# Block-causal attention and a gated MLP on one core: the order of every engine's steps is played out in the source

## The chip, the cores and the metric

The kernel runs on one core of a Trainium2 chip. The metric is the device time of one execution in microseconds (us); the comparison is with the kernel before the change. The core has five engines that run side by side, each through its own list of instructions, strictly in the order in which the program lists them: PE (TensorE, matrix products), DVE (VectorE), ACT (ScalarE), POOL (GpSimd), and SP (SyncE), which here does nothing but start DMA transfers. An instruction that needs another engine's result waits at the head of its engine's list, and all that stands behind it waits too.

## What is computed

First an attention over 8 batches, 8 heads, 576 positions and a head size of 64, where a position sees its own block of 64 positions and all blocks before it:

```
scores = (q @ k^T) / 8 ; masked where block(key) > block(query)
p = exp(scores - rowmax) / (rowsum + 1e-9)
x = p @ v                      # heads side by side: (8, 576, 512)
```

Then a gated MLP, one batch after the other:

```
h = relu(x @ w_in)             # 512 -> 1024; u = first half, v = second half
vn = (v - mean(v)) / sqrt(var(v) + 1e-6)
vs = w_spatial @ vn + b        # 576 x 576, mixes positions
out = (u * vs) @ w_out         # 512 -> 512
```

All inputs and outputs are fp32 (the two weight matrices of the MLP come as 64-bit floats and are converted on the chip). To be exact enough on a one-pass matmul format, most operands are split into a high and a low part, and a product is three matmuls: high by high, high by low, low by high. The attention scores of batch 0 alone are taken straight in fp32.

## The kernel before, in words

**Units of work.** Heads go in pairs, so the attention is 32 pairs (8 batches by 4), numbered 0 to 31. For one pair the kernel: loads the queries and keys (`load_pair`, one buffer `raw`) and the values (`load_v`); for batches 1 to 7 splits them into `hi` and `lo` (`prep_pair`, lines 242 and 245); makes scores on PE in seven slots of query tiles (`scores` L292 and `scores_last` L306); masks each score row, takes the row's extreme and moves it from PSUM to SBUF on DVE (`rows`, L337 and L355); takes exponentials on ACT with row sums (`exps`, L367); adds 1e-9 and takes the reciprocal on DVE (`norm`, L375 and L378) and scales the rows on POOL (L380). The probabilities must then be transposed. In batch 0 PE does it (`transposes`, L402, copied by ACT in L405); later DVE transposes 32 by 32 blocks (`blocks`, L415, four calls for a pair) and 16 DMAs put the blocks in place (`regroup`, L422). The product with the values follows on PE (`av`, L459, a low and a high part), its result is split by ACT and DVE (L439, L440), and POOL copies a tail of 64 positions (L480).

**The MLP.** `moe(b)` is a list of groups of matmuls, each group ending in one PSUM bank: 5 `v_group`s (L542, L555), 8 `u_group`s (L635, relu on ACT in L642), 8 `sp_group`s (L664 to L671, multiplied into u by DVE in L673, split by ACT in L674 and POOL or DVE in L677) and 8 output groups, made two at a time (`out_groups`, L697, copied out by ACT in L705 and stored by a DMA of SP's queue in L706). Behind each v group stands a chain that normalises its rows: relu on ACT (L549), statistics on DVE (L570, L571), logarithm and exponential on ACT (L574, L575), four small steps on DVE (`refine`, L578 to L590), the scaling (L596), the high part (L610) and the low part (L620) on DVE. The spatial product needs all five chains.

**What sets the order.** Batch 0's attention is a hand-written loop over steps of slots, with the conversions of the weights strewn in between (`spread`, `step_background`). From pair 4 on, the order comes from a small clock: every matmul of the MLP advances it by 133 or 230 ns (`M_NS`, `V_NS`, `tick`), and at fixed offsets from the start of a pair (the constants `ROWS_AT` to `V_AT`) events fire that list a step on DVE, ACT, POOL or SP. The scores stand at the start of a pair's period, the last scores at 4000 ns, the value product of the pair before at 13000 ns. The offsets are the same for all pairs and do not know how long any engine other than PE is busy. This order is fixed for PE, DVE, ACT and POOL (`tc.manual_schedule`, L849).

**Buffers.** Scores have six one-bank PSUM buffers and the MLP two. There is one buffer each for raw, hi and lo, one for the transposed probabilities, two for the untransposed ones, six for x.

## Time and profile before

| what | us |
|---|---|
| median of 3 runs | 769.93 (766.99 to 770.73) |
| the profiled execution | 768.27 |
| its span, from the first to the last instruction | 766.5 |
| PE busy in the span | 689.4 (90%) |
| DVE busy | 531.2 (69%) |
| ACT busy | 377.5 (49%) |
| POOL busy | 315.3 (41%) |

The span is what the engines' records cover; 1.8 us of the profiled execution lie outside it. Matmuls are pipelined: the record of one lasts about 0.3 us while the next starts 0.13 us after it, so PE counts as busy for a while after its last matmul has started, and PE busy at 90% does not mean that 90% of the matmuls that could have been done were done. The rows of the profile name a line of the kernel, an engine, the tile written and the tiles read; "<-" ahead of a name of an engine and a line means that this ended the wait.

### The profile page before, as it was taken

How to read it: one execution, taken by the hardware profiler on the slowest of the kernel's cores; microseconds unless marked ns; L12 is line 12 of the kernel's file. 1: busy time of each engine (PE TensorE's matmuls, PEld its weight loads, DVE VectorE, ACT ScalarE, POOL GpSimd, SP SyncE). 2: the span in 40 equal slices, each digit the busy share in tenths (PEclk: the TensorE clock that was granted, in tenths of full speed). 3: DMA queues.
4: the chain of work that ended last, by engine and by line, in shares of the span. 5: the costliest groups of instructions: out<-in, count | busy, mean ns of one | idle time of the engine just before them, and what ended most of it. 6: DMA issues, size and time to landing. Idle time of an engine off the chain costs nothing.

```text
span 766.5 us, 15461 instructions
## 1 busy us (share of the span) xinstructions
PE 689.4 (90%) x5320; PEld 596.0 (78%) x5320; DVE 531.2 (69%) x1609; ACT 377.5 (49%) x1068; POOL 315.3 (41%) x481
## 2 busy tenths in 40 slices
PE   8988678699999998989988999999988998987998
PEld 5656567688788886878878887888877887976897
DVE  7966979556975689657985679757985679741641
ACT  6774455444455545535555554444555454531322
POOL 5862476433354432544444532454444423530011
PEclk9989789989999999999999999999999999999999
DMA  6531454636446554456455544456446463334001
GB/s 220 179 130 34 118 174 125 167 103 172 108 118 165 153 137 105 115 152 160 108 133 152 144 131 127 119 144 169 110 122 166 113 160 95 93 86 117 1 16 47
DMA packets 42914, 95.56 MB, mean 125 GB/s; under 512 B 9554, under 2 KB 18258, under 8 KB 42836
## 3 DMA queue, kind: packets, MB, share of 16 engines
q1 hardware_dynamic: 42836, 94.58, 45.5%
q8 instruction: 42, 0.69, 0.4%
q14 instruction: 36, 0.29, 0.1%
HBM read 39.23 MB, written 9.44 MB: 63 GB/s over the span
## 4 chain that ended last, share of the span: by engine, by line
PE 42%; DVE 26%; SPq 10%; ACT 9%; DMA 7%; issue 4%; POOL 2%; DVEq 0%; ACTq 0%; POOLq 0%
PE ms L664 10%; SPq L422 9%; PE s_avh L459 7%; PE mv L542 6%; PE mu L635 6%; DVE p L415 5%; PE s L292 4%; PE mo L697 4%; ACT p L367 3%; DVE p L337 3%; PE s_avl L459 3%; DMA outT<-o 3%; ACT hi L242 2%; DVE vl L620 2%; DVE st L570 2%
## 5 line engine op out<-in xcount | busy, mean ns | idle before, releaser
L380 POOL TENSOR_SCALAR p<-p,ssum 128x128 f32<-128x128 f32 (+5 forms) x288 | 178.9, 635 | 252.5 <-DVE ssum L378 117.0
L367 ACT ACTIVATE p<-p,nmax 128x128 f32<-128x128 f32 (+5 forms) x288 | 169.1, 588 | 83.4 <-DVE nmax L337 53.2
L635 PE MATMUL mu<-x,wi_hi 128*128 128x288 f32 x512 | 119.8, 314 | 10.5 <-ACT u L642 9.4
L415 DVE STREAM_TRANSPOSE p<-p 128x768 f32<-128x768 f32 (+1 forms) x112 | 109.7, 992 | 1.2 <-POOL p L380 1.1
L635 PEld LDWEIGHTS mu<-x,wi_hi 128*128 128x128 f32 x512 | 91.9, 203 | 16.0 <-ACT u L642 11.3
L664 PE MATMUL ms<-ws_hi,vh 128*128 128x288 f32 x256 | 80.7, 315 | 21.2 <-ACT o L705 13.9
L542 PE MATMUL mv<-wi_hi,x 128*128 128x512 f32 x256 | 88.2, 404 | 4.2 <-ACT vr L549 4.2
L697 PE MATMUL mo<-gh,wo_hi 128*128 128x288 f32 x256 | 77.0, 301 | 5.4 <-ACT o L705 4.6
L664 PE MATMUL ms<-ws_lo,vh 128*128 128x288 f32 x256 | 78.0, 305 | 0.0
L664 PE MATMUL ms<-ws_hi,vl 128*128 128x288 f32 x256 | 77.7, 304 | 0.0
L337 DVE CUSTOM_DVE_ANT_1 p<-s,mask 128x128 f32<-128x128 f32 (+1 forms) x168 | 64.1, 413 | 17.1 <-PE s L292 14.3
L697 PE MATMUL mo<-gh,wo_lo 128*128 128x288 f32 x256 | 75.6, 295 | 0.0
L697 PE MATMUL mo<-gl,wo_hi 128*128 128x288 f32 x256 | 75.5, 295 | 0.0
L459 PE MATMUL s_avh<-pt,v 128*64 128x64 f32 (+2 forms) x1152 | 75.5, 285 | 0.0
L635 PE MATMUL mu<-x,wi_lo 128*128 128x288 f32 x256 | 75.0, 312 | 0.0
L674 ACT CAST gh<-u 128x288 fp32r<-128x288 f32 x64 | 27.1, 432 | 93.7 <-DVE u L673 85.6
L677 POOL TENSOR_TENSOR gl<-u,gh 128x288 fp32r<-128x288 f32 x48 | 38.2, 803 | 81.0 <-ACT gh L674 75.4
L664 PEld LDWEIGHTS ms<-ws_hi,vh 128*128 128x128 f32 x256 | 49.8, 195 | 27.6 <-ACT o L705 16.1
L673 DVE TENSOR_TENSOR u<-ms,u 128x288 f32<-128x288 f32 x64 | 27.8, 443 | 62.3 <-PE ms L671 62.1
L459 PEld LDWEIGHTS s_avh<-pt,v 128*64 128x64 f32 x1152 | 59.7, 140 | 14.2 <-issue 1.4
L245 POOL TENSOR_TENSOR lo<-raw,hi 128x320 fp32r<-128x320 f32 (+1 forms) x84 | 63.4, 779 | 2.7 <-ACT hi L242 2.6
L542 PEld LDWEIGHTS mv<-wi_hi,x 128*128 128x128 f32 x256 | 48.5, 190 | 16.8 <-ACT vr L549 5.4
(112 smaller groups left out, 1534.4 us busy)
## 6 DMA issues: line engine op xcount, KB each, us to landing
pt<-p SPq DMA_DIRECT2D x448, 100.0 KB, 2.2
raw<-qk SPq DMA_DIRECT2D x31, 640.0 KB, 4.4
v<-v SPq DMA_DIRECT2D x32, 320.0 KB, 3.0
outT<-o SPq DMA_DIRECT2D x64, 144.0 KB, 3.0
rwi<-w_in SPq DMA_DIRECT2D x8, 512.0 KB, 3.5
rwo<-w_out SPq DMA_DIRECT2D x4, 512.0 KB, 4.1
rws<-w_spT SPq DMA_DIRECT2D x4, 288.0 KB, 2.8
raw<-qk SPq DMA_DIRECT2D x2, 192.0 KB, 3.1
```

Source lines behind the costliest of these rows:

```text
L245: (nc.vector if n == 0 else nc.gpsimd).tensor_tensor(out=lo[:, cs], in0=raw[:, cs], in1=hi[:, cs].bitcast(F32), op=ALU.subtract)
L337: nc.vector.tensor_tensor_reduce(out=out, in0=by_block(b, bk[:, o:o + n]), in1=mask0[:, 512 - n:] if b == 0 else tiles(mask, 3 - t, t + 1) ...
L367: nc.scalar.activation(out, out, AF.Exp, bias=mx, scale=-1.0, accum_out=ssum[:, r:r + 1])
L380: nc.gpsimd.tensor_scalar(out=out, in0=out, scalar1=ssum[:, 4 + r:5 + r], scalar2=1.0, op0=ALU.mult, op1=ALU.mult,)
L415: nc.vector.transpose(pp, pp)
L422: nc.sync.dma_start(dst[32 * j:32 * j + 32, i], pp[32 * i:32 * i + 32, j])
L459: nc.tensor.matmul(bank[js, q0:q1], vt[:, c, js], move(j), start=(n == 0), stop=(n == len(todo) - 1), skip_group_check=True,)
L542: nc.tensor.matmul(ps, xs[k][:, j, cs], w[:, k, DH:], start=(n == 0), stop=(n == 3 * NC - 1),)
L635: nc.tensor.matmul(ps[:, :HT], w[:, k, ds], xs[k][:, j, zs], start=(n == 0), stop=(n == 3 * NC - 1),)
L664: nc.tensor.matmul(ps[:, :HT], a[:, ds], w[:, k, zs], start=(n == 0), stop=False)
L677: ).tensor_tensor(
L697: nc.tensor.matmul(ps[ec][:, :HT], w[:, k, es], a[:, k, :], start=(k == 0 and n == 0), stop=(last and n == 2),)
```

## The change

Every step of all engines, from the first load to the last store, is first put into one list (`Line.add`) with its engine, its length in ns, the steps that must be done before it (`after`; `behind` orders without a need for the result), the buffers that it takes and those that it gives back (`Ring`, `Hold`) and a rank. Then `Line.play` walks through time: at each turn every engine names the step that it could start earliest (`pick`; among those that could start at once, the lowest rank, then the oldest), the engine with the earliest start lists its step, its length is added to the engine's clock, and the steps that needed it are told when it ends. The order in which the steps come up is the order of the program on all five engines, SP among them.

PE has four lanes, each in fixed order (`pick_pe`): A the value products, T the transposes, S the scores, M the MLP. If several can start, A goes before T, T before S, S before M; `SLACK` counts an A as startable only 3000 ns after its data are there and an S 800 ns after (both 100 ns in batch 0), an M 100 ns after. `TURN` is a price in ns for going from one kind of work on PE to another. The scores of a pair from batch 1 on are held back until the MLP has gone far enough (`gate`, `LEAD` 5 pairs ahead).

Some steps are changed beside their order:
- 1e-9 is added to the row sums by POOL (`guard`) and no more by DVE; the reciprocal stays on DVE.
- `refine`, four small steps on DVE, becomes three on POOL.
- The high part of the normalised v is copied by ACT, no more by DVE.
- Relu of u, the copies of the output and batch 0's copies of transposed blocks go to ACT or DVE, whichever comes free first in the play.
- The score slots of both heads share one PSUM tile of two banks (three such tiles for six single ones). The order of the keys is moved by one tile so that the last slot's mask and extreme are one step on DVE instead of two, and the block transposes on DVE are seven calls for a pair instead of four.
- The output groups come one at a time; between the last spatial group of a half and its output groups stands a group that needs neither, and the last four output groups of a batch come after the first v group of the next.

The diff, cut to its core:

```diff
-RUN2, LAST = 2, 5
-
-
-ROWS_AT = [1000, 2600, 4200, 5600, 7000, 8600, 11000]
-EXP_LAG = 700
-NORM_AT = [5500, 8000, 11500, 13500]
-BLOCKS_AT = [9000, 12000, 15000, 16500]
-REGROUP_AT = 17500
-SPLIT_AT = 6000, 12000
-LAST_AT, OUT_AT = 4000, 13000
-STEP = 2860
-V_AT = [700, 1900, 2900, 3700, 4500, 5300]
-EARLY = OUT_AT - 3000
-V_NS, M_NS = 230, 133
-MOE_NS = 56 * V_NS + 304 * M_NS
+LEAD = 5.0
+
+TURN = {
+    ("M", "S"): 91, ("S", "M"): 384, ("S", "T"): 260, ("T", "S"): 200, ("S", "A"): 219,
+    ("A", "S"): 200, ("A", "M"): 250, ("A", "T"): 203, ("M", "A"): 96, ("T", "A"): 96,
+}
+REACH = {"PE": 170, "DVE": 125, "ACT": 145, "POOL": 70}
+SLACK = {"A": 3000, "S": 800, "T": 0, "M": 100}
...
+    def free_at(self, ahead=0):
+        k = len(self.given) + ahead - self.bufs
+        if k < 0:
+            return 0.0
+        if k >= len(self.given) or self.given[k].users:
+            return None
+        return self.given[k].freed
...
+    def start_of(self, op):
+        if op.left:
+            return None
+        at = op.ready
+        ahead = {}
+        for h in op.takes:
+            f = h.ring.free_at(ahead.get(id(h.ring), 0))
+            if f is None:
+                return None
+            ahead[id(h.ring)] = ahead.get(id(h.ring), 0) + 1
+            at = max(at, f)
+        return at
...
+    def pick_pe(self):
+        now = self.free["PE"]
+        heads = {k: q[0] for k, q in self.lanes.items() if q}
+        at = {k: self.start_of(op) for k, op in heads.items()}
+        if self.run and at.get(self.run) is not None:
+            return max(now, at[self.run]), heads[self.run]
+        at = {k: max(now, t + (SLACK[k] if heads[k].slack is None else heads[k].slack)) for k, t in at.items() if t is not None}
+        soon = [k for k in ("A", "T", "S", "M") if k in at and at[k] <= now + 1]
+        for k in soon:
+            op = heads[k]
+            if k == "S" and op.gate is not None and self.spent < op.gate and "M" in heads:
+                continue
+            return at[k], op
+        late = [k for k in at if not (k == "S" and heads[k].gate is not None and self.spent < heads[k].gate and "M" in at)]
+        if not late:
+            return None
+        k = min(late, key=lambda k: at[k])
+        return at[k], heads[k]
...
+    def pick(self, eng):
+        if eng == "PE":
+            return self.pick_pe()
+        now, best = self.free[eng], None
+        found = []
+        for op in self.open[eng]:
+            t = self.start_of(op)
+            if t is not None:
+                found.append((max(t, now), op))
+        if not found:
+            return None
+        first = min(t for t, _ in found)
+        return min(((t, op) for t, op in found if t <= first + 1), key=lambda x: (x[1].rank, x[1].turn))
...
+    def settle(self, op, at):
+        op.done = at
+        for h in op.drops:
+            h.users -= 1
+            h.freed = max(h.freed, at)
+        for heir in op.heirs + op.trail:
+            heir.left -= 1
+            if heir in op.heirs:
+                heir.ready = max(heir.ready, at)
+            if not heir.left and not heir.lane:
+                self.offer(heir)
...
+    def play(self):
+        while True:
+            picks = [(p[0], e, p[1]) for e in self.ENGINES for p in [self.pick(e)] if p]
+            if not picks:
+                break
+            start, eng, op = min(picks, key=lambda x: (x[0], self.ENGINES.index(x[1])))
+            for h in op.takes:
+                h.ring.given.append(h)
+            if len(op.eng) > 1:
+                op.fn(eng)
+            else:
+                op.fn()
+            ns = op.ns[op.eng.index(eng)]
+            if eng == "PE":
+                self.lanes[op.lane].pop(0)
+                kind = "M" if op.lane == "S" and op.waive else op.lane
+                end = start + TURN.get((self.kind, kind), 0) + ns
+                self.kind, self.run = kind, op.first and op.lane
+                if kind == "M" and op.lane == "M":
+                    self.spent += ns
+                done = end + REACH[eng]
+            else:
+                for e in op.eng:
+                    self.open[e].remove(op)
+            if eng == "SP":
+                end = start + ns
+                self.bus = max(self.bus, start + 300) + op.size / 240
+                done = self.bus + 1300
+            elif eng != "PE":
+                end = start + ns
+                done = end + REACH[eng]
+            self.free[eng] = end
+            self.last = eng, ns
+            self.settle(op, done)
...
-    ps_s = ctx.enter_context(tc.tile_pool(name="ps_s", bufs=6, space=PSUM))
+    ps_s = ctx.enter_context(tc.tile_pool(name="ps_s", bufs=3, space=PSUM))
     ps_m = ctx.enter_context(tc.tile_pool(name="ps_m", bufs=2, space=PSUM))
...
+        s_ops = []
+        pp_hold = Hold(r_pp, 7 if first else 16)
+        pt_hold = Hold(r_pt, 1)
+        s_hold = [Hold(r_s, n) for n in (4, 2, 2, 1)]
+        ns = (640, 640, 853, 960) if first else (670, 510, 690, 885)
+        for k in range(4):
+            op = add("PE", ns[k], (lambda k=k: scores(k)) if k < 3 else scores_last, after=need[k],
+                     takes=[s_hold[k]] + ([pp_hold] if k == 0 else []), lane="S",
+                     drops=([raw_hold] if first else [hl_hold] if k == 3 else []))
+            op.first = k < 2
+            op.waive = k == 3
+            op.slack = 100 if first else None
+            if k == 0 and not first:
+                op.gate = (g - LEAD) * MOE_NS / NPAIR
+            s_ops.append(op)
+
+        runs_of = [[] for _ in range(4)]
...
+            def guard(k=k, n=n):
+                s = box["sum", k]
+                nc.gpsimd.tensor_scalar(
+                    out=s[:, 0:n], in0=s[:, 0:n], scalar1=EPS_SM, scalar2=None, op0=ALU.add
                 )
...
+            def turn(k=k, n=n):
+                s = box["sum", k]
+                nc.vector.reciprocal(s[:, 4:4 + n], s[:, 0:n])
+
+            a = add("POOL", 200, guard, after=[e for *_, e in runs_of[k]], rank=2)
+            a = add("DVE", 165, turn, after=[a], rank=1.5)
...
+                cols = (P * ((t0, t1)[r] + 1)) if hd < 2 else S if first else Q0
+                muls[i].append(add("POOL", 240 + 0.825 * cols, scale, after=[a], rank=3))
...
-    def norm(b, pr, k):
-        ssum, runs = sums.pop((b, pr, k))
-        n = len(runs)
-        nc.vector.tensor_scalar(
-            out=ssum[:, 0:n], in0=ssum[:, 0:n], scalar1=EPS_SM, scalar2=None, op0=ALU.add
-        )
-        nc.vector.reciprocal(ssum[:, 4:4 + n], ssum[:, 0:n])
-        for r, out in enumerate(runs):
-            nc.gpsimd.tensor_scalar(
-                out=out, in0=out, scalar1=ssum[:, 4 + r:5 + r],
-                scalar2=1.0, op0=ALU.mult, op1=ALU.mult,
-            )
...
+                def blocks(t0=t0, t1=t1):
+                    x = box["pp"][:, :, t0:t1, :]
+                    nc.vector.transpose(x, x)
+
+                done.append(add("DVE", 70 + 1.05 * P * (t1 - t0), blocks, after=muls[i], rank=3))
...
+                    moved.append(add("SP", 635, regroup, after=done, drops=[pp_hold], rank=2, size=102400,
+                                     behind=moved[:1],
+                                     takes=[pt_hold] if not moved else []))
...
+        al = add("PE", 646, low_product, after=[*moved, got_v], takes=[a_hold], lane="A")
+        al.first = True
+        al.slack = 100 if first else None
+        ah = add("PE", 2082, high_product, behind=[al], lane="A", drops=[pt_hold, v_hold])
...
+            def refine(n):
+                st = box["st"]
+                if n == 0:
+                    nc.gpsimd.tensor_scalar(
+                        out=st[:m, 2:3], in0=st[:m, 7:8], scalar1=EPS_LN, scalar2=st[:m, 1:2],
+                        op0=ALU.add, op1=ALU.mult,
+                    )
+                elif n == 1:
+                    nc.gpsimd.tensor_scalar(
+                        out=st[:m, 3:4], in0=st[:m, 2:3], scalar1=st[:m, 1:2], scalar2=-0.5,
+                        op0=ALU.mult, op1=ALU.mult,
+                    )
+                else:
+                    nc.gpsimd.tensor_scalar(
+                        out=st[:m, 4:5], in0=st[:m, 3:4], scalar1=1.5, scalar2=st[:m, 1:2],
+                        op0=ALU.add, op1=ALU.mult,
+                    )
...
+            a = add("DVE", 800, stats, after=[a], rank=1.2)
+            a = add("ACT", 417, root, after=[a], rank=1)
+            for n in range(3):
+                a = add("POOL", 245, lambda n=n: refine(n), after=[a], rank=1)
+            a = add("DVE", 460, scale, after=[a], rank=1.2)
...
+            h = add("ACT", 520, high, after=[a], behind=vn_done[:1], takes=takes, rank=1.4)
+            l = add("DVE", 600, rest, after=[h], drops=[vr_hold], rank=1.4)
...
+                a = add(("ACT", "DVE"), (292, 360), copy, after=[ends[ec]], takes=[o_hold], drops=[holds[ec]], rank=0)
+                add("SP", 420, store, after=[a], drops=[o_hold], rank=0, size=P * HT * 4)
...
-            after(t + ROWS_AT[i], lambda i=i: do_rows(i))
-            after(t + ROWS_AT[i] + EXP_LAG, lambda i=i: exps(b, pr, i, kept[i]))
-        for k in range(4):
-            after(t + NORM_AT[k], lambda k=k: norm(b, pr, k))
-            after(t + BLOCKS_AT[k], lambda k=k: blocks(b, pr, k))
-        after(t + REGROUP_AT, lambda: regroup(b, pr))
...
+        sp = [lambda z=z, d=d: sp_group(z, d) for z in range(2) for d in range(ND)]
+        out = [lambda z=z, e=e: out_groups(z, (e,)) for z in range(2) for e in range(NO)]
+        front = [(vs if w == "v" else us).pop(0) for w in order]
+        return front[:1], front[1:] + sp[:ND + 1] + out[:NO] + sp[ND + 1:], out[NO:]
...
+    for b in range(B):
+        for pr in range(NPAIR):
+            attention(b, pr)
+    close = []
+    for b in range(B):
+        start, middle, end = moe(b, ready)
+        for group in start + close + middle:
+            group()
+        close = end
+    for group in close:
+        group()
 
...
+        line.play()
```

1207 lines of the change are left out of this document (597 added, 610 removed).

## The prediction

> **What bounds the kernel now.** I read the busy shares first, then the busy time by stage, then the distance between matmuls, and only then who waits for whom. The profiled execution took 768.27 us, 766.5 of them in the span; the median of the three runs is 769.93, so it is an ordinary execution, and the sum below is made against 768.27. About 0.5% either way is what a measurement of this kernel can tell from no change.
>
> ```profile
> span 766.5 us, 15461 instructions
> ...
> PE 689.4 (90%) x5320; PEld 596.0 (78%) x5320; DVE 531.2 (69%) x1609; ACT 377.5 (49%) x1068; POOL 315.3 (41%) x481
> ```
>
> PE leads, with DVE next. By stages (first column the stretch, then its length and the busy time of each engine, the granted clock of PE behind them): batch 0's attention, the start of the MLP beside batch 1's attention, the even middle, and the last batch's MLP alone.
>
> ```profile
> 0.00:61.00 61.00, 53.28 (x371) 34.74 (x371) 43.77 (x153) 43.28 (x121) 39.02 (x60) 0.94 0.49 166
> 61.00:180.00 119.00, 93.61 (x679) 82.63 (x677) 89.35 (x246) 58.44 (x160) 59.95 (x80) 0.89 0.48 129
> 180.00:705.00 525.00, 484.76 (x3882) 425.25 (x3880) 375.60 (x1151) 259.72 (x745) 211.23 (x334) 0.99 0.50 131
> 705.00:766.50 61.50, 57.72 (x400) 53.42 (x396) 22.52 (x59) 16.09 (x42) 5.11 (x7) 0.99 0.07 25
> ```
>
> A busy PE is not one at its peak, so I price its work by undisturbed runs of matmuls. The first four rows are from the chain of waits, the others from the timeline.
>
> ```profile
> 491.70 2.11 PE s L292 x24
> ...
> 711.12 1.58 PE mu L635 x12
> 712.70 2.77 PE mv L542 x12
> ...
> 759.77 3.07 PE mo L697 x21
> ```
>
> ```profile
> 484.41 0.87 PE L459 MATMUL s_avl<-pt,v 128*64 128x256 f32 x8
> ...
> 487.31 0.40 PE L664 MATMUL ms<-ws_hi,vl 128*128 128x288 f32 x1
> ```
>
> ```profile
> 495.96 0.31 PE L306 MATMUL s<-hi 128*128 128x320 f32 x1
> ...
> 496.70 0.31 PE L306 MATMUL s<-hi,lo 128*128 128x320 f32 x1
> ```
>
> A v matmul costs 2.77 / 12 = 0.231 us, every other one of the MLP 1.58 / 12 = 0.132. A batch has 4 x 12 + 8 = 56 of the first and 64 groups' worth, 304, of the second: 12.9 + 40.0 = 53.0 us. A pair's attention is 2.11 for scores, six last scores at (496.70 - 495.96) / 5 = 0.148, so 0.89, and 487.31 - 484.41 = 2.90 for the value product: 5.9. Going to other work and back costs by the change's own table 91 + 384 + 96 + 250 ns; less the 0.1 already inside 2.90 I take 0.7. That makes 6.6 us a pair and 53.0 + 4 x 6.6 = 79.4 a batch.
>
> PE's floor with the first 61 us as they are: 61 + 8 x 53.0 + 28 x 6.6 + 3.7 (from the last matmul, 759.77 + 3.07, to the end) = 673.5. So 93 us of the span are PE waiting, restarting or running at a lower clock behind its first 61 us. Where they lie:
>
> ```profile
> 526.49:614.32 87.83, 80.66 (x659) 70.62 (x656) 63.64 (x197) 44.79 (x129) 36.47 (x58) 1.00 0.51 134
> ...
> sum 526.95, PE 486.71 PEld 426.97 DVE 376.02 ACT 260.40 POOL 211.23; mean PE 81.12 PEld 71.16 DVE 62.67 ACT 43.40 POOL 35.20
> ```
>
> These are stretches of four pairs, from value product to value product, and the sum of all six from 178.35 to 705.30. One takes 87.8 where 79.4 are needed; all six lose 526.95 - 6 x 79.4 = 50.6. The stretch after 705.3 loses 61.2 - (2.2 of a value product + 53.0 + 3.7) = 2.3. What is left, 93 - 50.6 - 2.3 = 40, lies in the 117 us from 61 to 178, a third of that stage. The waits of PE, for 180 to 700 and then for 62 to 180:
>
> ```profile
> PE s L306 <- DVE nmax L337: 8.9, 8, 1.8
> PE ms L664 <- ACT o L705: 8.2, 5, 3.5
> PE ms L664 <- DVE u L673: 6.6, 8, 1.1
> PE mu L635 <- ACT u L642: 4.6, 6, 1.5
> PE mo L697 <- ACT o L705: 3.9, 8, 0.7
> ```
>
> ```profile
> PE ms L664 <- ACT o L705: 5.8, 1, 5.8
> PE s L306 <- DVE nmax L337: 5.5, 3, 2.2
> PE mu L635 <- ACT u L642: 4.9, 1, 4.9
> PE s L306 <- DVE st L578: 3.9, 1, 3.9
> PE mv L542 <- ACT vr L549: 3.0, 1, 3.0
> ```
>
> None of them is a lack of an engine's time over the span: in each case PE's list asks for something that ACT or DVE has further back in its own. They add to 32.2 and 23.1 us.
>
> **The change part by part.** *The middle.* Each wait has a place in the new order. The output copies are late because their store is:
>
> ```profile
> ACT o L705 <- DMA outT<-o: 30.9, 10, 7.1
> ...
> SPq L706 <- ACT o L705: 68.9, 21, 39.6
> ```
>
> ```profile
> 490.53 10.06 SPq L422 DMA_DIRECT2D pt<-p  x16
> 500.69 1.01 SPq L706 DMA_DIRECT2D outT<-o  x2
> ```
>
> Sixteen regroup issues occupy SP for 10 us and two stores go out right behind them. In the play a store has rank 0 and regroup rank 2, 635 ns an issue, so a store passes between two of them: of 8.2 + 3.9 I take 11 back. The last scores stand at a fixed 4000 ns; the play lists them 0.8 us after their bank is read: 8 of 8.9 back. The gating product and the relu get rank 0, the second may go to DVE: 4 of 6.6 and 3 of 4.6. The 18.4 that no row names are restarts and gaps of tenths; denser lists remove few: 4. Sum 30 of 50.6. Bounds: nothing, and all 50.6. I take the inner value because the lists are fixed and every length that is off comes back as a short wait.
>
> *The first MLP.* The same causes give 15 of 23.1 back. DVE is the engine that is short here (89.35 of 119 us, with PE waiting on it while it works through weights, v chains and transposes in the written order), and the play sends weights early and takes steps off it. Needed PE work is 117 - 40 = 77 us, and at 0.89 of the clock it lasts 77 / 0.89 - 77 = 9.5 longer; with fewer long gaps I take 5 back, and 4 of the rest: 24 of 40. Bounds 0 and 40. The Trainium skill (TensorE: Matmul & The Clock Gate, Part 1) says that the clock halves after an idle window of about 3.4 us and returns after a busy one of the same length. The waits of 5.8, 4.9 and 3.9 us beside 0.89 agree; by that rule all 9.5 would return as soon as no gap reaches that length, and the sum would be 4.5 us lower.
>
> *Batch 0.* ACT, DVE and POOL are busy 43, 44 and 39 of the 61 us, so none is full, and each pair's chain runs through all of them. The copies of transposed blocks may now go to DVE, but conversions of weights move in. Bounds: nothing, and 13 (the busiest engine's 44 plus 4 until the first data); I take 5. *The end* has one output group at a time with less to wait for: 1.
>
> *Steps taken off DVE.* The rows (busy us, mean ns) of the guard, the high part and two of the four steps of `refine`, and two POOL rows, the row scalings and the nearest to a small step:
>
> ```profile
> L375 DVE TENSOR_SCALAR ssum<-ssum 128x2 f32<-128x2 f32 (+2 forms) x128 | 22.6, 176 | 10.5 <-ACT p L367 10.2
> ...
> L610 DVE CAST vh<-vr 128x512 fp32r<-128x512 f32 x32 | 15.8, 493 | 0.4
> ...
> L582 DVE TENSOR_SCALAR st<-st 128x1 f32<-128x1 f32 (+1 forms) x40 | 10.9, 271 | 9.9 <-ACT st L575 6.7 <-DVE st L578 0.5
> L586 DVE TENSOR_SCALAR st<-st 128x1 f32<-128x1 f32 (+1 forms) x40 | 8.5, 213 | 1.4
> ```
>
> ```profile
> L380 POOL TENSOR_SCALAR p<-p,ssum 128x128 f32<-128x128 f32 (+5 forms) x288 | 178.9, 635 | 252.5 <-DVE ssum L378 117.0 <-DMA pt<-p 79.8 <-ACT p L367 33.5
> ...
> L480 POOL TENSOR_SCALAR xs<-x 128x128 fp32r<-128x128 f32 x32 | 10.0, 312 | 92.5 <-DVE ssum L375 68.0 <-DVE x L440 24.3
> ```
>
> These four alone free 58 us of DVE, so it is no bound. POOL gets 128 + 120 small steps. No row shows one; the nearest, 128 columns wide, takes 0.312, and nothing is the lower bound. At 0.312 they add 77 us to 315 (51% of the span), at 0.25, which I take for a step of 1 to 4 columns, 62. This is hidden by POOL's idle 60% in the middle. What isn't free is latency: each step stands behind POOL's row scalings in its list (635 ns), three times in a v chain. In batches 1 to 7 four u groups, 4 x 1.58 = 6.3 us, cover the last chain. Bounds per batch: 0 and 3 x 0.6 = 1.8; I take 0.3, so 2 us over the program. ACT gets the 32 casts, 16 us on 49%: nothing, under PE's work; without that cover half a us for each. The last slot's single reduction and three more transposes a pair cancel on DVE.
>
> Sum: -30 - 24 - 5 - 1 + 2 = -58. The span becomes 708.5, the execution 710.
>
> **The rivals.** *Everything waits in its place.* With 45 of 50.6, 34 of 40, 8 in batch 0 and 1 at the end it is 768 - 88 = 680. For it: no engine but PE is over 70% busy. Against it: the play knows nothing of an engine's disturbances.
>
> *The shared path of DVE and POOL.* The same DVE step at two times, and what POOL did at the second:
>
> ```profile
> 73.97 0.69 DVE L620 TENSOR_TENSOR vl<-vr,vh 128x512 fp32r<-128x512 f32 x1
> ...
> 87.89 1.77 DVE L620 TENSOR_TENSOR vl<-vr,vh 128x512 fp32r<-128x512 f32 x1
> ```
>
> ```profile
> 87.71 1.41 POOL L138 TENSOR_TENSOR ws_lo<-rws,ws_hi 128x576 fp32r<-128x576 f32 x1 [2.15 <-ACT ws_hi L136]
> ```
>
> It is held until POOL's subtraction is over: 1.08 us that no length in the change contains. A batch has some 13 such steps on DVE (5 scalings, 4 low parts of v, 4 of keys) and 18 subtractions on POOL. If half are held for a us and half of that reaches PE, it is 3.3 us a batch, 26 in all: 768 - 58 + 26 = 736. Against it: most steps of the profile show no such length. The Trainium skill (GPSIMD Engine Reference, 1. Specifications) says that GpSimd shares its SBUF interfaces with VectorE and collides with instructions of two SBUF inputs or in a two-port mode; the pair of rows agrees for the first kind, and by that rule a tighter packing brings more such meetings.
>
> *SP's list becomes the bound.* SP's order was not in the old fixed lists and is in the new. A store that waits for its ACT copy between regroup issues holds the rest, and PE's value product, fixed in its list, holds the MLP behind it. The play keeps 3.0 us of slack, so lateness beyond 3.0 us costs its excess 28 times; the gain is used up at 3.0 + 62 / 28 = 5.2 us for every pair, and at 6.0 the time is 768 - 58 + 28 x 3.0 = 794. For it: stores have waited up to 39.6 us at SP's head. Against it: then the copies were late themselves.
>
> *The lengths are wrong enough* that the new order waits as often as the old: 768.
>
> **How the numbers follow.** Forecast 710: 0.49, with its own range 696 to 724 (half the 30 and 24 lost or won in part). Everything in place, 680: 0.14. Shared path, 736: 0.24. No change: 0.04. SP, 794: 0.09. Faster by over 0.5% are the first three, 0.87; same 0.04; slower 0.09. The range from 684 to 748 leaves out about half of the second case, the two on the other side and the worst of the shared path.
>
> **What would show it.** Right: a stretch of four pairs falls from 87 to about 82 us; the waits for the output copy and for the last scores' bank go; stores stand between regroup issues; the clock from 61 to 180 is above 0.93; POOL's small steps take 0.2 to 0.3 us and DVE's busy time is below 480. Wrong: waits of PE for pt (then SP), DVE steps of over 1 us in numbers (shared path), or spatial products waiting for vl or st (the chain over POOL).

## The result and the profile after

The changed kernel takes 727.02 us (median of four runs, 725.46 to 730.96) against 770.33 (766.99 to 774.55) for the kernel before in the same comparison: a ratio of 0.9443, 95% interval 0.9383 to 0.9503. It is faster by 43 us where 58 to 60 were forecast. The time lies in the range given (684 to 748), but outside the 696 to 724 that the forecast of 710 had for itself, and nearer to the rival's 736. The profiled execution took 726.69 us, 724.9 of them in the span.

The span and the busy time of each engine, from the page of the profile after:

```profile
span 724.9 us, 15406 instructions
...
PE 668.6 (92%) x5320; PEld 585.1 (81%) x5320; DVE 501.3 (69%) x1397; ACT 361.7 (50%) x1013; POOL 384.0 (53%) x727
```

DVE lost 30 us of work and POOL gained 69, but the share of DVE did not fall, since the span became shorter. By stage (length, busy time and count of PE, its weight loads, DVE, ACT and POOL, then the granted clock and the share and GB/s of DMA), first before with the stages cut where the value product of batch 0, the start of batch 1's MLP and the start of the last MLP lie, then after:

```profile
61.00:180.40 119.40, 94.01 (x688) 82.96 (x684) 89.35 (x246) 58.44 (x160) 59.95 (x80) 0.89 0.48 130
180.40:708.20 527.80, 487.56 (x3909) 427.39 (x3907) 376.02 (x1152) 260.10 (x746) 211.23 (x334) 0.98 0.50 130
708.20:766.50 58.30, 54.52 (x361) 50.95 (x360) 22.09 (x58) 15.72 (x41) 5.11 (x7) 1.00 0.06 21
```

```profile
0.00:74.75 74.75, 56.29 (x399) 39.69 (x399) 54.90 (x171) 46.44 (x131) 55.44 (x89) 0.84 0.46 148
74.75:169.40 94.65, 82.50 (x648) 72.88 (x648) 73.77 (x192) 50.57 (x138) 63.76 (x105) 0.95 0.56 152
169.40:667.80 498.40, 475.95 (x3907) 421.07 (x3907) 351.46 (x992) 251.67 (x715) 256.77 (x515) 1.00 0.53 137
667.80:724.90 57.10, 53.90 (x371) 51.45 (x369) 21.12 (x44) 13.00 (x31) 8.00 (x18) 1.00 0.09 30
```

After the change the last four output groups of a batch (4 x 12 x 0.132 = 6.4 us) stand behind the next batch's first v group, so the cuts of the second table stand 6.4 us behind those v groups: the same work lies between the cuts of both. The middle went from 527.8 to 498.4, which is 88.0 to 83.1 us a batch and a gain of 29.4. The last MLP gained 1.2, the first 119.4 - 94.65 = 24.7. Batch 0's attention takes 74.75 where it took 61: a loss of 13.7. Together 41.6, all of the span's difference.

Who PE waits for in the middle (170 to 662 us; total, times, longest):

```profile
PE mu L919 <- ACT u L932: 7.3, 4, 2.2
PE mo L1008 <- DVE u L970: 5.8, 5, 2.0
PE s L532 <- DVE nmax L574: 3.8, 5, 1.2
PE av L714 <- DMA pt<-p: 1.2, 1, 1.2
```

The wait of the spatial product for the output copy, 8.2 us before, is gone, and that for the last scores' bank fell from 8.9 to 3.8. The wait for relu rose from 4.6 to 7.3, and gating's stayed at 6.6 in all (5.8 of it now ahead of the output product, 0.9 ahead of the spatial one). SP's list shows the stores between the regroup issues (start, duration, count):

```profile
146.40 1.16 SPq L696 DMA_DIRECT2D pt<-p  x2
147.63 0.55 SPq L1026 DMA_DIRECT2D outT<-o  x1
148.23 1.14 SPq L696 DMA_DIRECT2D pt<-p  x2
```

The small steps on POOL, the guard and the three of `refine`, have these durations (busy us, mean ns, idle before them):

```profile
L623 POOL TENSOR_SCALAR ssum<-ssum 128x2 f32<-128x2 f32 (+2 forms) x128 | 29.6, 231 | 157.9 <-ACT p L610 146.8 <-DMA pt<-p 2.9 <-PE mo L1008 1.9
...
L852 POOL TENSOR_SCALAR st<-st 128x1 f32<-128x1 f32 (+1 forms) x40 | 11.6, 291 | 75.1 <-ACT st L847 67.2 <-DVE u L934 6.4
...
L857 POOL TENSOR_SCALAR st<-st 128x1 f32<-128x1 f32 (+1 forms) x40 | 10.9, 272 | 3.1
L862 POOL TENSOR_SCALAR st<-st 128x1 f32<-128x1 f32 (+1 forms) x40 | 10.6, 266 | 3.3
```

**Where batch 0 loses.** Its last value product, in the chain of waits of before and of after (start, duration, matmuls):

```profile
59.28 1.81 PE s_avh L459 x32
```

```profile
71.02 3.73 PE av L714 x44
```

PE's waits of 0 to 75 us after the change:

```profile
PE t L665 <- ACT pt L296: 7.6, 4, 3.1
PE t L665 <- DVE pt L296: 5.3, 4, 2.6
```

The transposes wait for the copy that empties their bank; beside it the trace has 12.3 us in which their weight loads waited for a row scaling of POOL. POOL's scalings of 384 and 512 columns, in batch 0 and then in the middle:

```profile
L637 POOL TENSOR_SCALAR p<-p,ssum 128x384 f32<-128x384 f32 x10 | 9.1, 921 | 0.4
L637 POOL TENSOR_SCALAR p<-p,ssum 128x512 f32<-128x512 f32 x10 | 7.7, 778 | 0.0
```

```profile
L637 POOL TENSOR_SCALAR p<-p,ssum 128x512 f32<-128x512 f32 x46 | 34.4, 755 | 0.5
L637 POOL TENSOR_SCALAR p<-p,ssum 128x384 f32<-128x384 f32 x46 | 26.8, 590 | 0.5
```

The scalings of 384 columns are stretched from 590 to 921 ns, those of 512 hardly (755 and 778); the 40 scalings of up to 512 columns take 27.7 us in batch 0, a fifth more than the 22.8 that the means of the middle would give. And a scaling may stand late in POOL's list: by rank the conversions of the weights (1.8 to 2.4) go ahead of scalings (3) and of the copies of transposed blocks (2.5). The granted clock is lower too, 0.84 in this stage for 0.94 before: 0.16 x 74.75 = 12.0 us against 0.06 x 61 = 3.7, so by an estimate from these two rows up to 8 of the 13.7 us lost are clock.

### The profile page after: what moved, and what is told of

It reads as the page before. It is cut to its first block, busy times and chain, and to the rows that moved or that the text cites. A ratio compares the mean times of both kernels' runs of the same rounds, so it can differ in the third digit from the quotient of the medians.

```text
span 724.9 us, 15406 instructions
## 1 busy us (share of the span) xinstructions
PE 668.6 (92%) x5320; PEld 585.1 (81%) x5320; DVE 501.3 (69%) x1397; ACT 361.7 (50%) x1013; POOL 384.0 (53%) x727
## 4 chain that ended last, share of the span: by engine, by line
PE 46%; DVE 17%; DMA 9%; SPq 9%; POOL 8%; ACT 6%; issue 4%; ACTq 0%; POOLq 0%; DVEq 0%
PE mo L1008 9%; SPq L696 8%; PE av L714 8%; PE ms L956 7%; PE mu L919 6%; PE mv L809 6%; DMA raw<-qk 6%; DVE p L688 5%; POOL p L637 5%; PE s L514 4%; DVE p L574 4%; DMA pt<-p 3%; PE s L532 2%; ACT p L610 2%; DVE x L751 2%
## 5 line engine op out<-in xcount | busy, mean ns | idle before, releaser
L637 POOL TENSOR_SCALAR p<-p,ssum 128x128 f32<-128x128 f32 (+5 forms) x288 | 175.5, 622 | 23.2 <-DVE ssum L629 14.4
L688 DVE STREAM_TRANSPOSE p<-p 128x384 f32<-128x384 f32 (+2 forms) x196 | 122.1, 641 | 27.6 <-POOL p L637 26.7
L919 PE MATMUL mu<-x,wi_hi 128*128 128x288 f32 x512 | 112.8, 301 | 16.6 <-ACT u L932 15.4
L623 POOL TENSOR_SCALAR ssum<-ssum 128x2 f32<-128x2 f32 (+2 forms) x128 | 29.6, 231 | 157.9 <-ACT p L610 146.8
L919 PEld LDWEIGHTS mu<-x,wi_hi 128*128 128x128 f32 x512 | 86.2, 191 | 20.5 <-ACT u L932 16.6
L574 DVE CUSTOM_DVE_ANT_1 p<-s,mask 128x128 f32<-128x128 f32 (+1 forms) x224 | 94.8, 486 | 9.1 <-PE s L514 7.4
L714 PE MATMUL av<-pt,v 128*64 128x64 f32 (+2 forms) x1408 | 96.9, 294 | 3.5 <-DMA pt<-p 2.6
L714 PEld LDWEIGHTS av<-pt,v 128*64 128x64 f32 x1408 | 74.5, 139 | 29.4 <-issue 9.4
L956 PE MATMUL ms<-ws_hi,vh 128*128 128x288 f32 x256 | 77.1, 301 | 2.8 <-DVE u L970 2.8
L480 POOL TENSOR_TENSOR lo<-raw,hi 128x320 fp32r<-128x320 f32 (+1 forms) x84 | 70.5, 856 | 9.2 <-ACT hi L474 6.7
L919 PE MATMUL mu<-x,wi_lo 128*128 128x288 f32 x256 | 71.6, 301 | 0.0
L474 ACT CAST hi<-raw 128x640 fp32r<-128x640 f32 x56 | 39.5, 725 | 50.7 <-DMA raw<-qk 44.2
```

The lines of the kernel that those rows point to most:

```text
L474: nc.scalar.copy(box["hi"][:, cs], box["raw"][:, cs])
L480: eng.tensor_tensor(out=box["lo"][:, cs], in0=box["raw"][:, cs], in1=box["hi"][:, cs].bitcast(F32), op=ALU.subtract,)
L574: nc.vector.tensor_tensor_reduce(out=out, in0=by_block(b, bk[:, hd, o:o + n]), in1=mask0[:, 512 - n:512] if first else tiles(mask, 5 - t, ...
L637: nc.gpsimd.tensor_scalar(out=out, in0=out, scalar1=box["sum", k][:, 4 + c:5 + c], scalar2=1.0, op0=ALU.mult, op1=ALU.mult,)
L688: nc.vector.transpose(x, x)
L714: nc.tensor.matmul(box["av"][js, z, q0:q1], box["v"][:, c, js], move(j), start=(n == 0), stop=(n == len(todo) - 1), skip_group_check=True,)
```

## The experiments

Each run was timed beside the kernel before; differences from the changed kernel are differences of medians (727.02). In the profiled runs three numbers say where a run gained or lost: the starts of the value products of pairs 7 and 31, and between them the time for four pairs, which is one batch.

| run | median us | ratio to before (95%) | pair 7 | pair 31 | four pairs |
|---|---|---|---|---|---|
| kernel before | 770.33 | 1 | 177.5 | 703.8 | 87.7 |
| changed kernel | 727.02 | 0.9443 (0.9383 to 0.9503) | 160.0 | 658.5 | 83.1 |
| e1_batch0_first | 725.48 | 0.9399 (0.9339 to 0.9459) | 157.3 | 656.1 | 83.1 |
| e2_norm_on_dve | 737.82 | 0.9572 (0.9503 to 0.9642) | 157.0 | 666.0 | 84.8 |
| e3_old_order_norm_on_pool | 808.65 | 1.0479 (1.0413 to 1.0545) | 192.7 | 741.1 | 91.4 |
| e4_stores_late | 755.93 | 0.9781 (0.9707 to 0.9855) | 156.5 | 683.0 | 87.8 |
| e5_lengths_of_batch0 | 726.53 | 0.9437 (0.9382 to 0.9492) | 159.0 | 661.3 | 83.7 |
| e6_flat_lengths | 771.46 | 1.0029 (0.9994 to 1.0064) | 173.1 | 701.7 | 88.1 |
| e7_copies_on_act | 730.36 | 0.9483 (0.9432 to 0.9533) | 159.9 | 658.3 | 83.1 |
| e8_pairs4to7_first | 732.16 | 0.9512 (0.9465 to 0.9558) | 146.9 | 666.4 | 86.6 |
| e9_close_before_v1 | 724.26 | 0.9382 (0.9355 to 0.9409) | 161.9 | 655.7 | 82.3 |
| e10_less_slack | 739.35 | 0.9593 (0.9559 to 0.9627) | 155.4 | 670.4 | 85.8 |
| e11_refine_on_dve | 737.56 | 0.9551 (0.9510 to 0.9592) | 161.0 | 668.0 | 84.5 |
| e12_no_slack | 775.07 | 1.0058 (1.0032 to 1.0083) | 160.8 | 704.2 | 90.6 |

A kernel whose play has other lengths or ranks gets another order everywhere, so a difference is that of the whole list that comes out, not of one step alone.

**1. Is it the ranks that cost batch 0 its 13.7 us, and does the end get them back?** (`e1_batch0_first`)

```diff
-  muls[i].append(add("POOL", 240 + 0.825 * cols, scale, after=[a], rank=3))
+  muls[i].append(add("POOL", 240 + 0.825 * cols, scale, after=[a], rank=1.3 if first else 3))
...
-  moved.append(add(("ACT", "DVE"), ..., move, after=[a], drops=[h], rank=2.5, ...))
+  moved.append(add(("ACT", "DVE"), ..., move, after=[a], drops=[h], rank=0.5, ...))
```

> The changed kernel, but in batch 0 the row scalings on POOL get rank 1.3 (for 3) and the copies of transposed blocks rank 0.5 (for 2.5), so both stand ahead of the weights' conversions (1.8 to 2.4). Theory A (batch 0 grew from 61 to 75 us because its own chain ranks behind the weights): the last value product of batch 0 ends at 66 to 69 us for 74.7, and the median falls by 6 to 9 us, to about 719. Theory B (it grew because POOL's steps are held by DVE's conversions and because PE's clock drops, whatever the rank): under 2 us, 725 or more.

Batch 0's last value product ends at 64.6 us, 10 earlier: the ranks are most of the cause. The clock of the stage comes back with them (same columns as above):

```profile
0.00:64.59 64.59, 50.44 (x399) 35.73 (x399) 50.30 (x167) 43.24 (x124) 46.34 (x82) 0.95 0.46 152
```

By the same estimate 0.05 x 64.59 = 3.2 us are lost to the clock here for 12.0, so the ranks cost batch 0 much of their price through PE's clock. Theory B had the clock low whatever the rank; it is not. The total moved by 1.5, within the scatter of both: theory A is right on the place and wrong on the total, where theory B had the number. The ten microseconds go while the first MLP runs. PE's timeline at the value product of pair 7 (start, duration, count, then the idle time before it and what ended it), and the window around it:

```profile
157.29 5.60 PE L714 MATMUL av<-pt,v 128*64 128x256 f32 x44 [4.60 <-DMA pt<-p]
```

```profile
156.20:163.00 6.80, 5.71 (x45) 4.37 (x46) 4.26 (x8) 1.42 (x3) 5.72 (x8) 0.50 0.50 153
```

Pairs 4 to 7 come at 89.2, 120.2, 142.2 and 157.3, hardly ahead of the 93.7, 121.8, 143.4 and 160.0 of the changed kernel. Pair 7's product waits 4.60 us for its transposed probabilities and then runs at a granted clock of 0.50, in 5.60 us where the changed kernel takes 2.97. So the MLP of batch 1, which can't start before pair 7, starts at 162.83, where it started at 162.88. From there a batch takes 83.1 in both.

**2. Pairs 4 to 7 ahead of the weights as well** (`e8_pairs4to7_first`): the first run's edit, and rank 1.6 for scalings and block transposes of these pairs.

> The changed kernel with batch 0's steps ahead of the weights as in the first run, and with the row scalings and block transposes of pairs 4 to 7 ahead of the weights too (rank 1.6 for 3). Theory A (after batch 0 the next bound is the attention of pairs 4 to 7, whose regroup transfers came late, since their transposes rank behind the weights on DVE): the value product of pair 7 ends at 150 to 156 us for 163, and the median falls to 712 to 718. Theory B (the bound there is SP's list, where loads of weights wait for their staging buffers ahead of the regroup issues): within 3 us of the first run's 725.

Pair 7's value product starts at 146.9, 10 us earlier than in the first run, and the time is 7 us longer, which neither theory had. Now the weights are late. PE's longest wait from 75 to 220 us is for the output product's operand:

```profile
PE mo L1008 <- ACT gh L978: 5.4, 1, 5.4
```

The low part of the output weights is made from 121.7 to 154.7 us (106 to 128 in the changed kernel). The tile gh also holds weights on their way to conversion, and in batch 0 the source lists its first copy behind the output weights; it starts at 154.9. Pairs 8 and 9, whose ranks were left, follow at 174.2 and 210.0 (178.4 and 197.2 in the changed kernel). The stage up to pair 10 has two streams, weights and pairs, and here each was late when the other had the better rank. They share DVE, which in the changed kernel is full for a while in this stage:

```profile
100.00:120.00 20.00, 13.36 (x95) 12.68 (x96) 19.43 (x48) 10.63 (x30) 12.03 (x20) 0.83 0.56 151
```

**3. Did the first MLP's last outputs, listed behind pair 7, hold what batch 0 had gained?** (`e9_close_before_v1`): the first run's edit, and

```diff
-        for group in start + close + middle:
+        for group in (close + start if b == 1 else start + close) + middle:
```

> As the first run (batch 0's scalings and pt copies ahead of the weights), and batch 0's last four output groups stand ahead of batch 1's first value group in the MLP's list, so that they don't wait for pair 7. Theory A (the 10 us that batch 0 gained in the first run were lost because the last outputs of the first MLP stood behind pair 7): 718 to 722. Theory B (up to 170 us the weights and pairs 4 to 7 bound the time together, whatever the list of the MLP says): 724 to 727.

724.26, within 2 us of the first run: theory B. The outputs of the first MLP are done by 162 us and no longer by about 176, but pair 7 comes at 161.9 where it came at 157.3, and the work has again only swapped places. PE is busy 85.76 of the 96.75 us between the value products of pairs 3 and 7, at a granted clock of 0.91:

```profile
65.10:161.85 96.75, 85.76 (x614) 74.67 (x612) 75.61 (x194) 50.62 (x136) 69.78 (x106) 0.91 0.55 149
```

This is the fastest kernel seen, but its interval (0.9355 to 0.9409) overlaps with that of the changed kernel.

**4. Are batch 0's wrong lengths at fault?** (`e5_lengths_of_batch0`): the lengths in the play of weight conversions, batch 0's scores, transposes, value products and scalings set to what the trace after shows (later scalings and the guard get slightly longer too), as in

```diff
-  add("DVE", 600, merge, ...)          # 64-bit weights
+  add("DVE", 770, merge, ...)
-  add("POOL", 240 + 0.825 * cols, scale, ...)
+  add("POOL", (240 + 0.825 * cols) * (1.35 if first else 1.05), scale, ...)
```

> The changed kernel with other lengths in the play and nothing else: those that the profile after showed too short while batch 0 and the weights run (DVE's conversions 480, 400, 770, 770 ns for 340, 340, 600, 600; POOL's subtractions of weights 1.42 us for 1.23; the row scalings of batch 0 times 1.35; a PE transpose 160 ns for 108; the value product of batch 0 3.2 us for 2.7; scores of batch 0 some 12% longer). Theory A (batch 0 and the first MLP lose time because the lists were made with lengths that the chip does not keep there, so that every engine waits at the head of its list): 5 to 10 us faster, 716 to 722. Theory B (the lengths matter little; ranks and the resources themselves set these stages): within 3 us of the changed kernel.

726.53: no difference, theory B. Better lengths alone do not help; together with the ranks of the first run they were not tried.

**5. Do the lengths matter at all?** (`e6_flat_lengths`): in the play each DVE step is 350 ns long, each ACT step 360, each POOL step 500; PE and SP keep theirs. These are near the means of the profile after (501.3 / 1397 = 0.359 us, 0.357 and 0.528), so the load of each engine stays about the same in the play.

```diff
+        flat = {"DVE": 350, "ACT": 360, "POOL": 500}
+        self.ns = tuple(flat.get(e, n) for e, n in zip(self.eng, self.ns))
```

> The changed kernel, played with one length for every step of an engine (DVE 350, ACT 360, POOL 500 ns), PE's and SP's as they are. Theory A (the gain of the middle needs lists that know each step's length): 20 us slower or more, 745 or above. Theory B (what counts is the order of needs, buffers and ranks, and steps of one queue even out): within 8 us, 720 to 735.

771.46, a ratio of 1.0029 (0.9994 to 1.0064): the whole gain is gone, theory A with more than twice its least price. PE waits again (whole span; this kernel's lines stand two lower, so L921 is L919):

```profile
PE mu L921 <- DVE u L936: 14.3, 8, 2.5
...
PE ms L958 <- DVE u L972: 7.1, 6, 1.6
```

All other parts of the change are still in: ranks, two-bank score tiles, the merged last slot, steps moved to POOL and ACT. Together they are worth nothing here without lengths that tell the steps apart.

**6. Stores between the regroup issues** (`e4_stores_late`): rank 9 for stores instead of 0.

```diff
-  add("SP", 420, store, after=[a], drops=[o_hold], rank=0, size=P * HT * 4)
+  add("SP", 420, store, after=[a], drops=[o_hold], rank=9, size=P * HT * 4)
```

> The changed kernel with the output stores behind all other transfers in rank (9 for 0), so that they again go out behind the sixteen regroup issues. Theory A (the waits of PE for output copies, 12 us of the middle, went because stores pass between regroup issues): 8 to 12 us slower, about 737. Theory B (one group at a time and copies on two engines took those waits away): within 3 us of the changed kernel.

755.93, so 29 us back, where theory A had 8 to 12: the direction was right, the size was not. A batch takes 87.8 again. PE's waits over the span:

```profile
PE mu L919 <- ACT u L932: 18.3, 7, 7.8
PE av L714 <- DMA pt<-p: 12.9, 6, 3.2
PE ms L956 <- DVE o L296: 9.7, 4, 5.7
```

In the changed kernel these rows are 15.4, 2.6 and none. A late store holds the output tile, and the output copy behind it holds its engine (DVE's wait of o for the store, from 160 us to the last pairs, is 21.6 us where it was 11.1), so the bank that the copy frees comes late for the spatial product. Why pt comes later as well is not traced. The row of 8.2 us in the kernel before was no measure of this: the same lateness costs more in the new order.

**7. Small steps back to DVE, in the new order** (`e2_norm_on_dve`): guard and refine on `nc.vector`, with lengths of 165 and 215 ns.

> The changed kernel with the small norm steps (the guard and the three steps of refine) on DVE again, all else as it is, the order played anew with 165 and 215 ns for them. Theory A (these steps are worth next to nothing, at most the 2 us of latency forecast): 723 to 729. Theory B (the gain in the middle comes from taking them off DVE): 10 us slower or more, 737 or above.

737.82, 11 us slower than the changed kernel: the size of theory B. The forecast had put 2 us of cost on this move; it is worth 11 within the new order.

**8. Only refine back on DVE** (`e11_refine_on_dve`), the guard left on POOL.

```diff
-  nc.gpsimd.tensor_scalar(out=st[:m, 2:3], ...)     # and the two behind it
+  nc.vector.tensor_scalar(out=st[:m, 2:3], ...)
...
-  a = add("POOL", 245, lambda n=n: refine(n), after=[a], rank=1)
+  a = add("DVE", 215, lambda n=n: refine(n), after=[a], rank=1)
```

> The changed kernel with the refine steps (four for each 512-token norm) back on VectorE, the guard left on GpSimd. With both back it took 11 us more. Theory A (VectorE's load is what counts: the guard is about 29 us of VectorE's 40): 3 us more than the changed kernel, 728 to 732. Theory B (the refine steps in the chain to the value product count): 8 us more or above, 735 and over.

737.56: theory B. (The expectation speaks of four steps; the edit moves the three that the changed kernel has.) As far as the scatter tells (732.73 to 739.92), all 11 us are with refine's 120 steps (they take 33 us on POOL) and none with the guard's 128. PE's waits from 180 to 660 us, which were 3.8 and none in the changed kernel, while its waits of 7.3 for relu and 5.8 ahead of the output product are nearly gone (0.9 and none):

```profile
PE s L532 <- DVE nmax L574: 10.2, 7, 2.1
PE mv L809 <- DVE u L970: 9.3, 5, 2.2
```

How the first comes about shows in DVE's timeline at one of these places, and in PE's behind it:

```profile
382.44 0.17 DVE L842 BATCH_NORM_AGGREGATE st<-st 64x2 f32<-64x6 f32 x1
383.21 0.20 DVE L852 TENSOR_SCALAR st<-st 64x1 f32<-64x1 f32 x1 [0.59 <-ACT st L847]
383.45 0.21 DVE L857 TENSOR_SCALAR st<-st 64x1 f32<-64x1 f32 x1
383.69 0.20 DVE L862 TENSOR_SCALAR st<-st 64x1 f32<-64x1 f32 x1
383.93 0.54 DVE L869 TENSOR_SCALAR vr<-vr,st 64x512 f32<-64x512 f32 x1
384.39 0.28 DVE L574 CUSTOM_DVE_ANT_1 p<-s,mask 128x128 f32<-128x128 f32 x1
```

```profile
385.92 0.42 PE L532 MATMUL s<-hi 128*128 128x320 f32 x1 [2.11 <-DVE nmax L574]
```

The first refine step waits 0.59 us at DVE's head for ACT's exponential, the steps take 0.7 more, and the mask steps (L574), which free the bank of the last scores, stand behind: 1.3 of PE's 2.11 us. On POOL the same wait (67.2 us in all, in the rows of the profile after) costs PE nothing that its waits show. This is one path and not the whole cause: in run 7, with refine on DVE too and as slow, the wait for the last scores is 4.8 us, near the 3.8 of the changed kernel. The wait of mv is long in both (8.5 there). It is not explained by this: ahead of the first of these waits DVE's list had stood 2.64 us for ACT's high part of keys (1.66 in run 7), and whether the refine steps led to that order is not shown.

The Trainium skill (GPSIMD Engine Reference, 4.1 Engine selection) sends elementwise work to VectorE and says that GpSimd is about half as fast for two inputs and near line rate for one. The steps here have one input and widths of 1 to 4 columns; they take 231 to 291 ns on POOL and 175 to 212 on DVE in run 7, so POOL is slower by about a third, which agrees roughly, and the slower engine still was the better place by 11 us.

**9. The same move in the old order** (`e3_old_order_norm_on_pool`): the kernel before, with 1e-9 and its four refine steps on `nc.gpsimd`, in the places where they stood.

> The kernel before with its old order, and only the small norm steps (the guard and the four steps of refine) moved from DVE to POOL. Theory A: no gain by itself, 768 to 776 (the v chain gets longer by POOL's waits, up to 2 us a batch). Theory B (they are a part of the gain by themselves): 760 to 766.

808.65, 38 us slower than the kernel before, outside what either theory said. PE's waits, and what the guard waits for on POOL (last column of the row):

```profile
PE s L306 <- DVE nmax L337: 29.5, 15, 4.4
```

```profile
L375 POOL TENSOR_SCALAR ssum<-ssum 128x2 f32<-128x2 f32 (+2 forms) x128 | 31.3, 245 | 94.2 <-ACT p L367 78.1 <-DMA pt<-p 8.8
```

DVE has less to do (478.4 us) and PE waits twice as long for the bank that its masks free (14.4 us before). The guard now stands at POOL's head for ACT, DVE's reciprocal for the guard, and the masks behind the reciprocal for both. In the new order the guard waits on POOL even longer (146.8 us for ACT), but in the play nothing listed behind it could have started sooner. What waits for the guard is DVE: 70.9 us in this run, 23.3 in the changed kernel. Waiting is not all of the 38 us: the granted clock of the span is 0.936 where it was 0.967, which by 0.064 x 804 - 0.033 x 766.5 is up to 26 us of them.

**10. The choice between ACT and DVE for copies** (`e7_copies_on_act`): relu of u, output copies and batch 0's pt copies on ACT alone, as in

```diff
-  add(("ACT", "DVE"), (292, 360), copy, ...)
+  add("ACT", 292, copy_act, ...)
```

> The changed kernel with the relu of u, the output copies and batch 0's copies of transposed blocks on ACT alone, as before, and the order played anew. Theory A (the choice between ACT and DVE is a minor part): 2 to 6 us slower, about 731. Theory B (it is what took away the waits for output copies and banks): 12 us slower or more.

730.36, 3 us more, which the intervals do not tell apart; a batch takes the same 83.1. It is a minor part at most, theory A.

**11. Less slack, and none** (`e10_less_slack`, on top of the third run, and `e12_no_slack`, the changed kernel):

```diff
-SLACK = {"A": 3000, "S": 800, "T": 0, "M": 100}
+SLACK = {"A": 1500, "S": 400, "T": 0, "M": 100}     # e10
+SLACK = {"A": 0, "S": 0, "T": 0, "M": 0}            # e12
```

> The run before, with the slack that keeps value products and scores behind what they read cut from 3 us (AV) to 1.5 and to 0.4 for scores. Theory A (the slack only pushes products late): 3 to 5 us faster than the run before. Theory B (the slack covers real lateness of regroup and norm): TensorE waits for pt or p, 5 us or more slower than it.

> The changed kernel with every slack at zero: each TensorE step is played at the time its inputs are reckoned ready. If the slack covers real lateness, TensorE's waits for pt, p and u grow by 15 us or more together and the time is 740 or above; if it only delays, 722 to 728.

739.35 and 775.07: the third run lost 15 us and the changed kernel 48, its whole gain. Both sizes are those that were expected of a slack that covers real lateness (theory B of the first); the path is another one with half the slack. With half the slack PE hardly waits for pt (1.9 us from 180 to 660). It is ACT that waits, for PE. ACT's waits after the change, with less slack and with none (three views; 25.9 in the third run):

```profile
ACT x L748 <- PE av L714: 31.3, 20, 3.9
```

```profile
ACT x L748 <- PE av L714: 87.0, 31, 7.7
```

```profile
ACT x L748 <- PE av L714: 108.0, 31, 6.3
```

The play believes that the value product is early and lists its split on ACT early. The product comes late, the split stands at ACT's head, the relu behind it, and PE waits for the relu: mu for u 12.9 us from 180 to 660, where the third run has 4.1 and the changed kernel 7.3. With no slack PE's own wait is there too:

```profile
PE av L714 <- DMA pt<-p: 29.4, 18, 3.3
```

So the slack is not room that could be had. The longest of these waits, 3.3 us, is near the slack of 3 us; that 3 us is the best size is not shown, and each of the two runs changed the slack of scores along with that of value products.

## Why the prediction was right, and where it was not

The forecast of 710 was 17 us too low. The direction, the range and the gain of the middle held. Luck has a part in it: the first MLP met its number for other reasons, and the range was wide enough for a loss in batch 0 that its bounds did not have.

- **The middle, -30:** measured -29.4. Of its parts the output copy's wait (11 with its half in the output product) went as said, and the late stores cost 29 us when put back, which is their price in the new order and not in the old one. The last scores gave 5 of the 8 taken. Gating gave nothing (6.6 before; 5.8 and 0.9 after, most of it now ahead of the output product), the relu's wait rose from 4.6 to 7.3. What made up for these is the 18.4 that no row was said to name, of which I gave back 4. It was read wrongly. The sum of 32.2 took five rows; the shorter rows of that view, and a wait of 3.6 at 703.8, after its end, make it 39.6, so 11 of the 50.6 had no wait to them. And these were no gaps of tenths but clock, most of them: in five stretches of 3.4 us of the trace before, from 211.9, 474.7, 648.8, 679.5 and 703.4, PE's granted clock is 0.50 (one row below). PE is busy 15.66 us in them, of which full speed would have saved at most half, 7.8. After the change one such stretch is left, and of the 22 us still lost (6 x (83.1 - 79.4)) the listed waits are all. So the six stretches of four pairs gained about 17 us of listed waits and up to 6 of clock, for which the sum had no term here; the other 5 of their 28 have no row.

```profile
211.90:215.30 3.40, 3.40 (x16) 3.40 (x16) 3.09 (x11) 1.58 (x6) 0.42 (x2) 0.50 0.69 163
```

- **The first MLP, -24:** -24.7, but not for the reasons given. The stage is shorter mostly because it starts 13.7 us later and still hands over where pairs 4 to 7 let it: put together with batch 0, it is 11 us shorter. The match of 24 and 24.7 is luck. The clock rose from 0.89 to 0.95, as said. From 100 to 120 us it is 0.83, beside one wait of PE for the relu of 8.2 us (that relu stands on ACT behind copies that wait for DVE); the Trainium skill (TensorE: Matmul & The Clock Gate, Part 1) gives an idle window of about 3.4 us as the cause of a lower clock, and the trace agrees here. It does not everywhere: in batch 0 no wait of PE is over 3.1 us, and from 20 us on the clock is 0.77 to 0.83. So the clock does not come back as soon as no gap reaches that length, and here the measurement decides.
- **Batch 0, -5: the step that failed.** It took +13.7, outside the bounds (nothing, and a gain of 13), which had no loss in them. The prediction saw that conversions of weights move in and that no engine is full, and took that for room. It did not read the ranks, by which POOL and DVE serve the weights first whenever both could start, on a chain that runs through every engine, nor did it have a clock that falls as that chain makes PE wait (0.84, and 0.95 with the other ranks). The first run shows that 10 of these us are the ranks. The remaining 3.5 are not traced.
- **Two terms that don't add.** Batch 0 and first MLP were summed as -5 and -24; both end in one event, the value product of pair 7 with all weights ready. Together they gave 119.4 + 61 to 74.75 + 94.65, a gain of 11 where 29 were forecast. These 18 are more than the whole difference between forecast and measurement in the span, 58 - 41.6 = 16.4. The first run gives batch 0 back 10 us and the end 1.5; e8 and e9 move pairs, weights and outputs against each other and the end stays. What sets this stage's length is shown only as far as this: two streams share DVE, POOL and SP, and putting one ahead delays the other. Whether an order exists that shortens both stays open.
- **The end, -1:** 1.2.
- **Small steps on POOL, +2:** the durations were right (0.23 to 0.29 against 0.25 taken), the sign was wrong: the move is worth 11 us in the new order, all with refine. "DVE is no bound" was right, and not the question: a step with a wait at its head costs what stands behind it in the list. One such place was traced in run 8 (1.3 of 2.11 us); what makes up the rest of the 11 us stays open. DVE's busy time fell to 501, not below 480.
- **The shared path of DVE and POOL (736):** small in the middle. The low part of v there takes 0.68 us in the median and never over 0.69 (0.69 and up to 1.17 before); the scaling ahead of it rose in the mean from 561 to 648 ns, with single ones of 1.14, which is 2 us over 23 steps. From 97 to 105 us, beside POOL's low part of keys, low parts of v take 1.08 and 1.13. In batch 0 POOL's scalings of 384 columns are stretched by half (921 against 590 ns), those of 512 hardly (778 against 755), while DVE converts weights; which of DVE's steps holds them is not shown. The Trainium skill (GPSIMD Engine Reference, 1. Specifications) names collisions of this kind, and the rows of 384 columns fit it. The forecast was missed in the stages up to pair 7, which is where such stretched steps stand. What they cost there is not shown, so for these stages the rival is not settled.
- **SP's list as the bound (794):** PE waits 1.2 us for pt in the middle. The slack of 3 us covers it, as runs e10 and e12 show from the other side: at zero slack the time is 775. (With the gain of 58 the break-even of this rival is 3.0 + 58 / 28 = 5.1 us, not 5.2; the 62 has no source.)
- **Lengths wrong (768):** not so, but with flat lengths the time is 771, near the rival's price.

## What to carry to other kernels

An order made by playing out all steps is worth what its lengths and its slack are worth: with flat lengths (44 us) or without slack (48 us) the gain was gone, while correcting lengths by about a third in the start-up stage changed nothing. When a step moves to another engine, price what stands behind it in that list and how long it may wait at the head, and not only its duration and the engine's busy share: nearly the same move was 11 us better in one order and 38 worse in the other. Price PE's waits with its clock: half or more of what batch 0 lost, and of those 38 us, can be clock. Terms of stages that end in the same event are one term; find that event (here pair 7 and the weights) before giving each of them a gain.

## What was unexpected of the hardware

A wait of PE can cost more than its length, and it need not be long. In the changed kernel a wait of 2.08 us is followed by 3.4 us at a granted clock of 0.50, with 17 matmuls in them and 31 in the 3.4 us behind:

```profile
205.40 0.40 PE L919 MATMUL mu<-x,wi_hi 128*128 128x288 f32 x1 [2.08 <-ACT u L932]
```

```profile
205.80:209.20 3.40, 3.40 (x17) 3.40 (x16) 2.36 (x5) 0.75 (x3) 1.04 (x1) 0.50 0.54 123
209.20:212.60 3.40, 3.40 (x31) 3.23 (x32) 1.44 (x4) 1.18 (x3) 0.78 (x3) 1.00 0.58 137
```

Not every such wait does this: from 160 to 658 us PE waits 24 times, and this is the only fall of the clock. What decides is not shown.

A row scaling of 384 columns on POOL took 921 ns on average in batch 0 and 590 in the middle, with the same form and the same tiles; before the change it was the other way round, 703 and 804. Sixteen regroup issues keep SP for 10 to 11 us where they stand together, and one store put between them takes 0.55; a regroup lands 2.2 us after its issue in the median, so in this kernel the last of sixteen lands late mostly by the time of issuing. In batch 0 the granted clock after the change is 0.77 to 0.83 from 20 us on, and the same value product of 44 matmuls takes 2.92 us at one place there and 4.14 at another:

```profile
42.56 2.92 PE av L714 x44
...
53.10 4.14 PE av L714 x44
```
